# Two small tensors allocated ahead of the load ring of a one-token attention and MLP kernel

## The chip, the core and the metric

The kernel runs on one core of a Trainium2 chip, with the other cores idle. The metric is the device time of one execution in microseconds (us). The time before is the median of three runs, 2518.27 us, the lowest 2518.11 and the highest 2518.29.

The engines of the core are called PE (matrix multiplication; PEld is its weight load), DVE (vector), ACT (scalar), POOL and SP. SP does no arithmetic here: it issues the loads, which 16 DMA engines carry out. On-chip memory is SBUF, 128 partitions side by side, and PSUM, into which PE accumulates.

## What is computed

One token passes through an attention block with a cache of 65536 keys and values for each of 32 heads, and through a gated MLP; a gate mixes both.

```
q = (x @ wq) as 32 heads of 128
scores = q . k_cache * 128**-0.5          (32 heads x 65536 keys)
o = softmax(scores) . v_cache             (32 heads x 128)
a = o @ wo
b = (silu(x @ w_gate) * (x @ w_up)) @ w_down
g = sigmoid(sum(x * gate_w))
out = g * a + (1 - g) * b
```

All tensors are bf16. k_cache and v_cache hold 32 x 65536 x 128 elements each, 537 MB, and every byte of them is read once. The weights add 13.9 MB.

## The kernel before

**The ring.** One SBUF tensor, `ring` (line 74), takes all large loads: 176 KiB in each partition, cut by byte offsets into places. The first half of a head's K lies at K_A (0) and the second at K_B (32 KiB); with 64 KiB each they lie at 0 to 64 and at 32 to 96 KiB, so each is loaded into what the other has left. The two halves of V lie at V_A (96 KiB) and V_B (112 KiB) in the same way. wq comes first, at 144 KiB; wo, w_gate, w_up and w_down reuse the places of K at the end. `at(byte, n)` (line 119) gives the part of the ring from a byte offset on; all offsets are multiples of 256 bytes.

**The loads.** Each half of a head's K or V is 8 MiB: 256 rows of 128 bf16 in each of 128 partitions, that is one contiguous run of 64 KiB per partition in HBM and in SBUF. SP issues them in one queue, in the order written out at lines 142 to 197: for each head K's first half of the next head, V's second half, K's second half, V's first half, each after a wait for the engine that frees the place (`ktd` for K, counted up by DVE; `va1` and `vbd` for V, counted up by PE). In the first head K comes in four loads of 4 MiB. In the last, V's second half comes in six parts (PARTS, line 123), the first of them ahead of a wait for `va1`, and w_down in one large load and three small ones that follow the parts of V.

**The computing.** DVE transposes K chunk by chunk (`turn`, line 310; L314) from the ring into one of four buffers of `kt`, 16 chunks per half-head; PE multiplies each with the head's q, laid out in `zq` (L401), into scores in the bank psS. After a head's last chunk DVE takes the maximum (L338), POOL the maximum over the partitions (L216), ACT the exponential (L251), DVE transposes the weights into `pb` (L340), and PE multiplies V by them (L417 and L408). At the end come wo (L428 and L512), the MLP (L488 and after) and the sum into one row.

**The two small tensors.** `om` (line 85, 64 bytes per partition) holds the last-but-one set of attention outputs as weights for wo; ACT writes it once (L259), PE reads it in 32 matmuls (L428). `qTb` (line 97, 64 bytes per partition) holds q in bf16; ACT writes it once (L239), and PE reads it in 4 matmuls (L395).

**Where tensors lie.** SBUF tensors are laid out in the order in which `sb` (line 56) is called, one after the other, behind a scratch area of 16384 bytes and four small constants of 32 bytes each per partition. So `ring`, which is called first, begins at byte 16384 + 128 = 16512 of each partition.

## Time and profile before

| | |
|---|---|
| median of three runs | 2518.27 us |
| the profiled execution, its own time | 2518.01 us |
| its span, from first to last instruction | 2516.6 us |
| read from HBM | 1087.64 MB, 432 GB/s over the span |
| loads into the ring | 144, of which 125 are of 8 MiB |

The profile has a page with the busy times of the engines, the DMA queues and the chain of work that ended last, and a trace that can be asked for windows, waits and DMA packets. A DMA packet is one run of bytes into one partition; DMA share is the mean busy share of the 16 DMA engines. Chain rows give a start and a duration in us, and what took it. Rows of windows give the stretch and its length, then for each engine the busy time and the number of instructions, then the granted clock of PE as a share of full speed, the DMA share and the rate. In rows of groups come the line, engine and operation, what is written from what, the count, then the busy time, the mean of one in ns, and the idle time ahead of them with what ended it.

### The profile page before, as it was taken

What the parts mean: (1) busy time and instruction counts of PE and PEld (TensorE: products, weight loads), DVE (VectorE), ACT (ScalarE), POOL (GpSimd) and SP (SyncE); (2) the same over time, 40 slices, a digit from 0 to 9 for tenths busy, and PEclk for the clock granted to TensorE, in tenths of its full rate; (3) what the DMA queues carried; (4) which work ended last, traced back from release to release, by engine and by line L of the source; (5) the groups of instructions that cost most, each with busy time, mean ns of one, the idle gap of its engine ahead of it and who ended that gap; (6) DMA issues with size and microseconds to landing.
All of it is one profiled execution on the core that took longest, in us unless ns stands there. A gap on an engine that the chain in (4) does not pass through costs nothing.

```text
span 2516.6 us, 25250 instructions
## 1 busy us (share of the span) xinstructions
PE 1511.9 (60%) x10158; PEld 573.9 (23%) x10158; DVE 1249.7 (50%) x1213; ACT 43.0 (2%) x142; POOL 25.9 (1%) x81
## 2 busy tenths in 40 slices
PE   4565655745656556566565575565655655656568
PEld 1222222212222222222222121222212222212222
DVE  5454553644545536445455364464553644545534
ACT  0000000000000000000000000000000000000000
POOL 0000000000000000000000000000000000000000
PEclk8877877878778778778787787877877778778788
DMA  9999999999999999999999999999999999999999
GB/s 419 434 433 433 434 433 434 433 434 434 434 433 434 434 433 435 433 432 433 433 433 433 433 433 433 433 433 433 433 434 433 433 433 434 433 433 433 433 432 394
DMA packets 20748, 1087.73 MB, mean 432 GB/s; under 512 B 2307, under 2 KB 2694, under 8 KB 2950
## 3 DMA queue, kind: packets, MB, share of 16 engines
q1 hardware_dynamic: 20736, 1087.64, 99.9%
q8 instruction: 4, 0.07, 0.0%
q14 instruction: 2, 0.02, 0.0%
q10 hardware_dynamic: 6, 0.00, 0.0%
HBM read 1087.64 MB, written 0.00 MB: 432 GB/s over the span
## 4 chain that ended last, share of the span: by engine, by line
DMA 75%; DVE 15%; issue 7%; PE 2%; DVEq 1%; SPq 0%; ACT 0%; POOL 0%
DMA ring<-in_A_k_cache_dram 74%; DVE kt L314 15%; PE psS L401 2%; DMA ring<-in_A_v_cache_dram 1%; DVEq L311 0%; SPq L145 0%; PE psW L417 0%; DVE st L325 0%; PE psY L423 0%; ACT pa L251 0%; DVE pb L340 0%; DVE st L338 0%; DVEq L324 0%; DVE fin L359 0%; SPq L136 0%
## 5 line engine op out<-in xcount | busy, mean ns | idle before, releaser
L401 PE MATMUL psS<-kt,zq 128*128 128x512 bf16 x4096 | 1132.6, 425 | 854.6 <-DVE kt L314 835.3
L314 DVE STREAM_TRANSPOSE kt<-ring 128x1024 uint32<-128x1024 uint32 x1024 | 1163.1, 1206 | 939.7 <-DMA ring<-in_A_k_cache_dram 939.7
L401 PEld LDWEIGHTS psS<-kt,zq 128*128 128x128 bf16 x4096 | 385.1, 104 | 1588.3 <-DVE kt L314 1129.7
L417 PE MATMUL psW<-ring,pb 128*4 128x512 bf16 x3584 | 256.2, 448 | 102.7 <-DVE pb L340 102.4
L417 PEld LDWEIGHTS psW<-ring,pb 128*4 128x4 bf16 x3584 | 94.8, 98 | 262.6 <-issue 187.8
L327 DVE COPY brow<-psW 128x512 f32<-128x512 f32 x32 | 22.1, 691 | 120.5 <-PE psW L417 120.5
L408 PEld LDWEIGHTS psO<-pb,ring 128*128 128x128 bf16 x2048 | 57.0, 98 | 0.5 <-DMA ring<-in_A_v_cache_dram 0.2
L408 PE MATMUL psO<-pb,ring 128*128 128x1 bf16 x2048 | 56.6, 163 | 0.2
L330 DVE TENSOR_SCALAR lt<-psO,st,sc 128x4 f32 x32 | 9.4, 294 | 89.1 <-PE psO L408 89.1
L452 PE MATMUL psO<-id,brow 128*128 128x1 f32 x256 | 33.8, 253 | 25.5 <-DVE brow L327 24.7
L340 DVE STREAM_TRANSPOSE pb<-pa 128x512 bf16<-128x512 bf16 x32 | 22.8, 711 | 48.7 <-ACT pa L251 48.7
L249 ACT ACTIVATE st<-st 128x1 f32<-128x1 f32 x32 | 6.5, 203 | 2358.5 <-POOL st L216 2358.5
L338 DVE TENSOR_REDUCE st<-psS 128x1 f32<-128x512 f32 x32 | 22.1, 692 | 37.4 <-PE psS L401 37.4
L452 PEld LDWEIGHTS psO<-id,brow 128*128 128x128 f32 x256 | 31.0, 191 | 41.7 <-DVE brow L327 40.4
L216 POOL PARTITION_ALL_REDUCE st<-st x32 | 11.2, 351 | 2420.2 <-DVE st L338 2420.2
L251 ACT ACTIVATE pa<-psS,st 128x512 bf16<-128x512 f32 x32 | 22.0, 687 | 1.0
L428 PE MATMUL psF<-ring,om 128*1 (+1 forms) x32 | 12.7, 396 | 2.9 <-DMA ring<-in_A_wo_dram 2.9
L512 PE MATMUL psY<-ring,hot 128*128 (+1 forms) x32 | 13.1, 411 | 0.0
L218 POOL PARTITION_ALL_REDUCE st<-st x32 | 12.3, 383 | 36.4 <-ACT pa L251 36.4
L256 ACT COPY zq<-qd 128x16 bf16 x31 | 7.7, 248 | 0.0
L251 ACT ACTIVATION_READ_ACCUMULATOR pa<-psS,st 128x1 f32 x32 | 6.2, 193 | 0.0
L428 PE MATMUL psF<-ring,kt 128*1 128x512 bf16 x11 | 4.2, 564 | 3.0 <-DVE kt L353 3.0
(87 smaller groups left out, 52.8 us busy)
## 6 DMA issues: line engine op xcount, KB each, us to landing
ring<-in_A_k_cache_dram SPq DMA_DIRECT2D x4, 4096.0 KB, 27.4
ring<-in_A_v_cache_dram SPq DMA_DIRECT2D x3, 2048.0 KB, 17.6
ring<-in_A_wq_dram SPq DMA_DIRECT2D x1, 4096.0 KB, 12.4
ring<-in_A_wo_dram SPq DMA_DIRECT2D x2, 2048.0 KB, 10.6
ring<-in_B_w_gate_dram SPq DMA_DIRECT2D x1, 1792.0 KB, 21.4
ring<-in_B_w_up_dram SPq DMA_DIRECT2D x1, 1792.0 KB, 25.4
ring<-in_B_w_down_dram SPq DMA_DIRECT2D x1, 1408.0 KB, 13.1
ring<-in_A_v_cache_dram SPq DMA_DIRECT2D x1, 1280.0 KB, 20.4
```

Of the source, the lines that this page charges most:

```text
L218: nc.gpsimd.partition_all_reduce(Lt, rsum, P, RADD).then_inc(sm["s_L"], 1)
L251: nc.scalar.activation(pa[:], psS[:], ACT.Exp, bias=nbias, scale=SCALE, accum_out=rsum).then_inc(sm["s_exp"], 1)
L314: nc.vector.transpose(o, src).then_inc(sm["ktd"], 1)
L327: nc.vector.tensor_copy(brow[:], psW[:]).then_inc(sm["s_flc"], 1)
L338: nc.vector.reduce_max(mxs, psS[:], AX_X).then_inc(sm["s_mx"], 1)
L340: nc.vector.transpose(pb[:], pa[:]).then_inc(sm["s_pb"], 1)
L401: last = nc.tensor.matmul(psS[:], zw[je][c], ktb[n % NB][:, je // 2, :, je % 2], start=first and je == 0, stop=stop and je == 3)
L408: last = nc.tensor.matmul(psO[:, 0:1], at(base + r * 256, Dh), pb[:, col:col + 1], start=first and n == 0, stop=stop and n == len(rows) - 1)
L417: last = nc.tensor.matmul(psW[g:g + 4, :], pb[:, col:col + 97:32], at(base + r * 256, 4 * Dh), start=first and n < 4, stop=stop and n >= l ...
L428: return nc.tensor.matmul(psF[0:1, :], lhs, rhs, start=first, stop=stop)
L452: nc.tensor.matmul(psO[:, 0:1], brow[:, e * Dh:(e + 1) * Dh], id4[:, e:e + 1], start=e == 0, stop=False)
L512: return nc.tensor.matmul(psY[:], hot[:, bass.ds(31 - j, P)], w, start=first, stop=stop)
```

## The change

`om` and `qTb` are allocated ahead of `ring` instead of behind it. With 64 bytes each in a partition they move the ring from byte 16512 to byte 16640 of each partition. The tensors from `kt` to `hot` move by 128 bytes too, those from `o31` to `xTz` by 64, and `hbuf` and `st` keep their place. The instructions of all engines, their order and their waits are the same; only addresses differ.

```
+        om = sb("om", [P, 32], BF16)
+        qTb = sb("qTb", [P, H], BF16)
         ring = sb("ring", [P, RING // 2], BF16)
...
         hot = sb("hot", [P, P + 32], BF16)
-        om = sb("om", [P, 32], BF16)
         o31 = sb("o31", [P, 2], BF16)
...
         xTz = sb("xTz", [P, 4 * 32], BF16)
-        qTb = sb("qTb", [P, H], BF16)
         hbuf = sb("hbuf", [P, 5, 16], F32)
```

More of the change, by code (lines that the diff above doesn't have):

```diff
@@ L72, in bass_gated_mix__mha_block_cached__swiglu_ffn__decode_kernel @@
         psF = psum("psF", [P, 512], F32)
+        om = sb("om", [P, 32], BF16)
+        qTb = sb("qTb", [P, H], BF16)
         ring = sb("ring", [P, RING // 2], BF16)
@@ L84, in bass_gated_mix__mha_block_cached__swiglu_ffn__decode_kernel @@
         hot = sb("hot", [P, P + 32], BF16)
-        om = sb("om", [P, 32], BF16)
         o31 = sb("o31", [P, 2], BF16)
@@ L96, in bass_gated_mix__mha_block_cached__swiglu_ffn__decode_kernel @@
         xTz = sb("xTz", [P, 4 * 32], BF16)
-        qTb = sb("qTb", [P, H], BF16)
         hbuf = sb("hbuf", [P, 5, 16], F32)
```

## The prediction

> **What bounds the kernel now.** I read the page's first lines, its waits and its chain, then the DMA answers for chosen windows.

> ```profile
> span 2516.6 us, 25250 instructions
> PE 1511.9 (60%) x10158; PEld 573.9 (23%) x10158; DVE 1249.7 (50%) x1213; ACT 43.0 (2%) x142; POOL 25.9 (1%) x81
> DMA  9999999999999999999999999999999999999999
> DMA packets 20748, 1087.73 MB, mean 432 GB/s; under 512 B 2307, under 2 KB 2694, under 8 KB 2950
> q1 hardware_dynamic: 20736, 1087.64, 99.9%
> DMA 75%; DVE 15%; issue 7%; PE 2%; DVEq 1%; SPq 0%; ACT 0%; POOL 0%
> ```

> The 16 DMA engines are busy from end to end, with one queue, q1, which holds all loads that SP issues. No compute engine passes 60%. The chain that ended last is three quarters DMA; the rest of it is DVE, PE and issue time in which the chain has stepped over to the work that released the next load, while the DMA engines stayed busy with the one before. That they stayed busy shows in the steady part, taken as six equal windows, of which the first and the last stand here (PE, PEld, DVE, ACT, POOL, then granted clock, DMA share and GB/s):

> ```profile
> 100.00:487.00 387.00, 228.72 (x1565) 89.05 (x1563) 193.66 (x186) 5.65 (x20) 3.67 (x10) 0.77 1.00 434
> 2035.00:2422.00 387.00, 230.87 (x1565) 87.56 (x1563) 193.64 (x186) 5.64 (x20) 3.67 (x10) 0.78 1.00 434
> ```

> So the time of the steady part is (bytes through q1) / (rate of q1), and only what changes that rate can move it. The waits say the same from the other side:

> ```profile
> DVE kt L314 <- DMA ring<-in_A_k_cache_dram: 939.7, 65, 22.6
> SPq L145 <- DVE kt L314: 1369.6, 65, 30.7
> ring<-in_A_v_cache_dram SPq DMA_DIRECT2D x63, 32.4
> ring<-in_A_k_cache_dram SPq DMA_DIRECT2D x62, 29.3
> ```

> DVE idles 939.7 us for K, 14.5 us in each of its 65 waits. SP too waits a great deal before it issues, but a load lands 29.3 or 32.4 us after its issue, and its own bytes need 19.35 us (worked out next): each load is issued some 10 us before its turn, and the queue does not run dry.

> The exact rate comes from two rows of the chain of waits, both K loads of the same phase of a head:

> ```profile
> 62.44 29.26 DMA ring<-in_A_k_cache_dram
> 2268.47 29.23 DMA ring<-in_A_k_cache_dram
> ```

> Between them lie 57 half-heads, each with one K and one V load of 8 MiB: (2268.47 - 62.44) / 57 = 38.702 us for 16.777 MB, 433.5 GB/s. One load takes 19.351 us, and in it each of the 16 DMA engines writes 8 packets of 64 KiB and one small packet that raises the semaphore (q1 has 20736 packets = 144 loads x (128 + 16); the 16 x 144 = 2304 small ones are nearly all of the 2307 under 512 B).

> **How much of a packet is not its bytes.** A change of start address can touch what a packet costs beside its bytes. The trace gives that by comparing long packets with short ones. At the end the queue moves rows of 1 KiB:

> ```profile
> DMA packets 126, 0.11 MB, mean 36 GB/s; under 512 B 16, under 2 KB 126, under 8 KB 126
> q1 hardware_dynamic: 126, 0.11, 10.5%
> ```

> This is the window from 2512.9 to 2516 us: 110 packets of 1 KiB and 16 small ones took 10.5% of 16 x 3.1 us = 5208 ns. With a cost c for each packet and a rate r of one engine, 126c + 112640/r = 5208 here, and 9c + 524288/r = 19351 in the steady part. The solution is c = 8.5 ns and r = 27.2 bytes per ns. The 10.5% is rounded, which leaves c open by 0.2 ns. So of the 2419 ns from one 64 KiB packet to the next, 2409 are bytes and 8.5 are c.

> **The change part by part.**

> *The ring.* In the built programs' tables of tensors the ring begins at byte 16512 of each partition before (64 x 256 + 128) and at 16640 after (65 x 256). Every load into it starts at a whole multiple of 256 bytes from the ring's start (16 K, 32 K, r0*256, 1024j), so before the change every data packet begins 128 bytes into a 256-byte block and ends 128 bytes into another; afterwards each one covers whole blocks. The same 144 loads with the same packets are issued, behind the same waits; no instruction is added, removed or reordered on any engine, SP's queue among them.

> No row of before shows a load into an aligned ring, so the gain per packet is bounded from two sides. One end is nothing: c may have no part that depends on the address. The other is the whole c, 8.5 ns. I take 4.7 ns, close to the middle: the time that the 128 unused bytes of the first block would need at r, 128 / 27.2. That is the cost if a packet that begins inside a block pays for the whole block. Below nothing, I bound it by the same amount with the other sign (in the rivals).

> [...]

> How many packets count: each load puts 8 data packets on each engine. The last three loads (1 KiB rows of w_down) are issued behind the last part of V and are not what the chain waits for. That leaves 141 x 8 = 1128 packets in a row on each engine. Gain: 1128 x 4.7 ns = 5.3 us; the ends are 0 and 1128 x 8.5 ns = 9.6 us.

> *Does the gain reach the end?* In the steady part yes: the queue always has the next load, and 0.04 us less per load (8 x 4.7 ns) is nothing beside the 10 us of lead. In the tail SP has to wait for PE before it issues the last parts of V:

> ```profile
> 2432.53 29.84 DMA ring<-in_A_k_cache_dram
> 2484.96 5.32 PE psW L417 x37
> 2492.09 21.33 DMA ring<-in_A_v_cache_dram
> 2513.46 0.37 PE psO L408 x8
> 2492.00:2493.00 1.00, 1.00 (x12) 0.27 (x8) 0.00 (x0) 0.00 (x0) 0.00 (x0) 1.00 1.00 424
> ```

> The last K load lands at 2462.4; compute then sets the moment of that issue, 2490 to 2492. It moves forward with the landing of K, by the 1048 packets before it (131 loads x 8), 4.9 us. In the meantime the engines work off the loads already queued, five of them with 40 packets each engine (V's first half, w_gate, w_up, w_down, the first part of V's second half), which now end 0.2 us earlier relative to K. They are still at full share at 2492, and from there 21.3 us pass until the last part lands, of which the 48 KiB per partition issued there need 14.5 us: some 5 us of older work is ahead of them. So the queue still does not run dry, and the full 5.3 us arrive at the landing at 2513.4. The 3.2 us from there to the end stay.

> *The other moved tensors.* kt, zq, qd, pa, pb, lt, ident, sel, ramp and hot move by 128 bytes, o31 to xTz by 64, and om and qTb to the front. All moves are multiples of 64 bytes, the shapes stay.

> ```profile
> L314 DVE STREAM_TRANSPOSE kt<-ring 128x1024 uint32<-128x1024 uint32 x1024 | 1163.1, 1206 | 939.7 <-DMA ring<-in_A_k_cache_dram 939.7
> L401 PE MATMUL psS<-kt,zq 128*128 128x512 bf16 x4096 | 1132.6, 425 | 854.6 <-DVE kt L314 835.3
> L428 PE MATMUL psF<-ring,om 128*1 (+1 forms) x32 | 12.7, 396 | 2.9 <-DMA ring<-in_A_wo_dram 2.9
> ```

> I cost these at nothing. The cover is DMA: the transposes may lengthen by a tenth (16 x 0.12 = 1.9 us in a half-head) and still fit in the 14.5 us that DVE waits there. If the cover were gone, that tenth would cost 64 x 1.9 = 123 us, so a shift of this kind would be seen at once in the mean of L314. The matmuls that read om are 12.7 us in all, while the last K load and V's first half are in flight; a tenth of them would be 1.3 us.

> *The sum.* Profiled execution: span 2516.6, 2518.0 with the 1.4 us around it. 2516.6 - 5.3 + 1.4 = 2512.7. The median of the three runs is 2518.3, 0.3 above the profiled one, so the forecast for the median is 2513.0 us. With 0.5 ns of doubt on the 4.7 its own range is 2512.4 to 2513.6.

> **The rivals.**

> *Nothing changes.* c is a packet's own cost, whatever its address. For it speaks the small packet that raises a semaphore, seen alone in the 20 ns from 2516.17 us:

> ```profile
> q10 hardware_dynamic: 1, 0.00, 2.8%
> ```

> 2.8% of 16 x 20 ns is 9.0 ns for 4 bytes, which need 0.15 ns at r. It has nothing to do with the ring and costs as much beside its bytes as a data packet does. Against it: a write of 4 bytes fills its own block only in part too, so it may pay in the same way. Time: 2518.3, with 0.3 either way.

> *The whole c goes.* A packet that starts and ends inside blocks may pay at both ends, and twice 4.7 ns is already more than c. Then 9.6 us are saved: 2518.3 - 9.6 = 2508.7. Against it: some time between two packets is needed for any address, as the semaphore's packet suggests.

> *Slower: the blocks are counted from another origin.* The offset is counted from the start of a partition. If a partition's first byte stood 128 bytes into a block of the memory that DMA writes, the ring would be aligned today and misaligned by the change. Place: the first block of each data packet; price: 128 / 27.2 = 4.7 ns on each, c becomes 13.2; it decides from the first load on, since nothing hides the queue: 2518.3 + 5.3 = 2523.6. For it: nothing in the trace shows the origin, and a c of 8.5 ns can be had without any misalignment, as the semaphore's packet shows. Against it: the partition's 16 KiB and the tensors' offsets are all counted from zero, and a start at an odd 128 would be a strange one.

> **How the numbers follow.** Half a block saved, 0.55; nothing, 0.25; the whole c, 0.10; slower by half a block, 0.10. The likeliest gives 2513.0. The range takes in nothing and the bound of c: 2508.5 to 2518.8, which leaves out the slower case and little else. A change of 0.2% is 5.0 us (about what a measurement of this kernel can tell from no change), so the line runs at 2513.2, just above the forecast: of the first case I count three quarters as faster. Faster 0.42 + 0.10 = 0.52; same 0.13 + 0.24 = 0.37; slower 0.11.

> **What would show it.** If right, K loads in the chain stand 38.626 us per half-head apart instead of 38.702 (two loads, 16 packets, 4.7 ns each), the same pair of rows 4.3 us closer, the 1 KiB window gives a c near 3.8 ns, the first K load lands less than 0.1 us earlier (16 packets), and DVE's and PE's mean durations at L314 and L401 stay. If the pitch stays at 38.70, c is the packet's own. If the pitch shrinks and the time does not, the gain is lost in the tail between 2462 and 2492. What would make all of it wrong is a change in r itself, above all a pitch that moves by more than 0.14 us per half-head, which c cannot give.

## The result and the profile after

The changed kernel takes 2513.71 us (median of 21 runs, 2513.45 to 2514.49), against 2518.29 us in 21 runs of the kernel before (2518.03 to 2519.19). The ratio is 0.9982, with a 95% interval of 0.9975 to 0.9988: 4.6 us faster. The forecast was 2513.0, a gain of 5.3 us. The median lies 0.1 us above the range of the forecast's own case (2512.4 to 2513.6) and inside the whole range (2508.5 to 2518.8).

The page of the changed kernel, with the span, the DMA packets, the queue and two groups (busy time, mean in ns | idle time before them):

```profile
span 2512.5 us, 25250 instructions
DMA packets 20749, 1087.73 MB, mean 433 GB/s; under 512 B 2308, under 2 KB 2695, under 8 KB 2951
q1 hardware_dynamic: 20736, 1087.64, 100.0%
L401 PE MATMUL psS<-kt,zq 128*128 128x512 bf16 x4096 | 1132.7, 426 | 851.7 <-DVE kt L314 833.2
L314 DVE STREAM_TRANSPOSE kt<-ring 128x1024 uint32<-128x1024 uint32 x1024 | 1163.1, 1206 | 936.4 <-DMA ring<-in_A_k_cache_dram 936.4
```

The queue q1 moves the same number of packets as before (20736), the transposes and matmuls are as long as before (1206 ns, 426 against 425), and DVE waits 3.3 us less for K. Only the queue has become faster. By how much is read in the chain of waits, from issues of K an even number of half-heads apart. The time per half-head is called the pitch:

```profile
62.40 29.18 DMA ring<-in_A_k_cache_dram
139.63 29.54 DMA ring<-in_A_k_cache_dram
178.66 29.11 DMA ring<-in_A_k_cache_dram
217.19 29.29 DMA ring<-in_A_k_cache_dram
2226.38 29.26 DMA ring<-in_A_k_cache_dram
2265.12 29.11 DMA ring<-in_A_k_cache_dram
```

From 217.19 to 2226.38 lie 52 half-heads: a pitch of 38.638 us. Before, the even pair is 62.44 and 2229.72, the latter in the next fence:

```profile
2191.07 29.22 DMA ring<-in_A_k_cache_dram
2229.72 29.27 DMA ring<-in_A_k_cache_dram
2268.47 29.23 DMA ring<-in_A_k_cache_dram
```

This gives 2167.28 / 56 = 38.701 us. The reader should take pairs an even number apart, because half-heads alternate: 38.65 and 38.75 us before (the last three rows), 38.53 and 38.74 after. The prediction called its pair, 57 apart, one of the same phase; it isn't, and that cost it 0.001 us.

The gain is 0.063 us per half-head, 3.9 ns on each of the 16 packets. By the medians it is 4.58 us / 1128 packets = 4.06 ns. The span of the profiled execution shrank by less, 4.1 us. Part of the rest stands in the rows above: the half-head from 139.63 took 39.03 us, against 38.74 in the run with a pad ahead of the ring, shown below, whose addresses are as good. So it is a matter of this execution.

The tail of the chain in the changed kernel:

```profile
2428.91 29.82 DMA ring<-in_A_k_cache_dram
2481.32 4.48 PE psW L417 x48
2487.61 21.73 DMA ring<-in_A_v_cache_dram
2509.38 0.36 PE psO L408 x8
```

The last K lands at 2458.7 instead of 2462.4, V's last part at 2509.3 instead of 2513.4, and 3.2 us remain after it as before. Nothing of the gain is lost there: the last stretch gains some 0.4 us more than K's landing did.

### The profile page after: what moved, and what is told of

Same layout as the page of the kernel before. It is cut to its first block, busy times and chain, and to the rows that moved or that the text cites. A ratio compares the mean times of both kernels' runs of the same rounds, so it can differ in the third digit from the quotient of the medians.

```text
span 2512.5 us, 25250 instructions
## 1 busy us (share of the span) xinstructions
PE 1510.1 (60%) x10158; PEld 574.4 (23%) x10158; DVE 1249.7 (50%) x1213; ACT 43.0 (2%) x142; POOL 25.9 (1%) x81
## 2 busy tenths in 40 slices
DMA  9999999999999999999999999999999999999999
DMA packets 20749, 1087.73 MB, mean 433 GB/s; under 512 B 2308, under 2 KB 2695, under 8 KB 2951
## 3 DMA queue, kind: packets, MB, share of 16 engines
q1 hardware_dynamic: 20736, 1087.64, 100.0%
HBM read 1087.64 MB, written 0.00 MB: 433 GB/s over the span
## 4 chain that ended last, share of the span: by engine, by line
DMA 75%; DVE 15%; issue 7%; PE 2%; DVEq 0%; SPq 0%; ACT 0%; POOL 0%
DMA ring<-in_A_k_cache_dram 74%; DVE kt L314 15%; PE psS L401 2%; DMA ring<-in_A_v_cache_dram 1%; DVEq L311 0%; SPq L145 0%; PE psW L417 0%; DVE st L325 0%; PE psY L423 0%; ACT pa L251 0%; DVE pb L340 0%; DVE st L338 0%; DVEq L324 0%; DVE fin L359 0%; SPq L136 0%
## 5 line engine op out<-in xcount | busy, mean ns | idle before, releaser
L401 PE MATMUL psS<-kt,zq 128*128 128x512 bf16 x4096 | 1132.7, 426 | 851.7 <-DVE kt L314 833.2
L314 DVE STREAM_TRANSPOSE kt<-ring 128x1024 uint32<-128x1024 uint32 x1024 | 1163.1, 1206 | 936.4 <-DMA ring<-in_A_k_cache_dram 936.4
L401 PEld LDWEIGHTS psS<-kt,zq 128*128 128x128 bf16 x4096 | 386.8, 104 | 1583.9 <-DVE kt L314 1120.7
L417 PE MATMUL psW<-ring,pb 128*4 128x512 bf16 x3584 | 253.5, 444 | 103.5 <-DVE pb L340 102.4
L417 PEld LDWEIGHTS psW<-ring,pb 128*4 128x4 bf16 x3584 | 93.9, 97 | 261.3 <-issue 184.4
L408 PEld LDWEIGHTS psO<-pb,ring 128*128 128x128 bf16 x2048 | 56.8, 98 | 0.6 <-DMA ring<-in_A_v_cache_dram 0.6
L408 PE MATMUL psO<-pb,ring 128*128 128x1 bf16 x2048 | 56.5, 163 | 0.4 <-DMA ring<-in_A_v_cache_dram 0.2
L428 PE MATMUL psF<-ring,om 128*1 (+1 forms) x32 | 13.1, 410 | 2.7 <-DMA ring<-in_A_wo_dram 2.7
L428 PE MATMUL psF<-ring,kt 128*1 128x512 bf16 x11 | 4.0, 542 | 2.9 <-DVE kt L353 2.9
## 6 DMA issues: line engine op xcount, KB each, us to landing
ring<-in_A_wo_dram SPq DMA_DIRECT2D x2, 2048.0 KB, 10.5
```

The costliest lines, as they stand in the source:

```text
L314: nc.vector.transpose(o, src).then_inc(sm["ktd"], 1)
L401: last = nc.tensor.matmul(psS[:], zw[je][c], ktb[n % NB][:, je // 2, :, je % 2], start=first and je == 0, stop=stop and je == 3)
L408: last = nc.tensor.matmul(psO[:, 0:1], at(base + r * 256, Dh), pb[:, col:col + 1], start=first and n == 0, stop=stop and n == len(rows) - 1)
L417: last = nc.tensor.matmul(psW[g:g + 4, :], pb[:, col:col + 97:32], at(base + r * 256, 4 * Dh), start=first and n < 4, stop=stop and n >= l ...
L428: return nc.tensor.matmul(psF[0:1, :], lhs, rhs, start=first, stop=stop)
```

## The experiments

The runs that differ by a pad are the kernel before with an unused tensor of so many bytes per partition, ahead of the ring where nothing else is said. Prices per packet are taken against 2513.71 us, with 1128 packets.

**The ring by a pad.** The pad moves the ring, and everything behind it by the same 128 bytes; `om` and `qTb` stay behind the ring.

```
+        pad = sb("pad", [P, 64], BF16)
         ring = sb("ring", [P, RING // 2], BF16)
```

> The ring moves by 128 bytes behind an unused pad, with om and qTb where they were; all tensors behind the ring move by 128 too. Theory (the ring's place alone does it): the time of the changed kernel, 2513.7 us, steady pitch of K loads 38.64 us per half-head. Rival (om or qTb at the front matter): 2518.3 or between.

Measured: 2513.64 us, ratio 0.9982 (0.9973 to 0.9991). Its chain:

```profile
62.50 29.19 DMA ring<-in_A_k_cache_dram
139.71 29.26 DMA ring<-in_A_k_cache_dram
178.45 29.09 DMA ring<-in_A_k_cache_dram
2226.12 29.26 DMA ring<-in_A_k_cache_dram
2264.87 29.11 DMA ring<-in_A_k_cache_dram
2428.67 29.64 DMA ring<-in_A_k_cache_dram
```

2163.62 / 56 = 38.636 us per half-head, and here from the start on (139.71 to 178.45 is 38.74). Any 128 bytes would do in the place of `om` and `qTb`: their own new place does nothing.

**The rest alone.** The same pad, behind the ring.

```
         ring = sb("ring", [P, RING // 2], BF16)
+        pad = sb("pad", [P, 64], BF16)
         kt = sb("kt", [P, NB, CH * 64], U32)
```

> The pad stands behind the ring: the ring stays at 128 bytes into a block, all tensors behind it move by 128. Theory (the ring's place): no gain, 2518.3 us, pitch 38.70. Rival (kt, zq or another tensor behind the ring gains by its multiple of 256): 2513.7, or a mean of L314 or L401 that moves.

Measured: 2518.15 us, ratio 0.9998 (0.9989 to 1.0007), and this chain:

```profile
62.80 29.29 DMA ring<-in_A_k_cache_dram
2230.10 29.28 DMA ring<-in_A_k_cache_dram
```

2167.30 / 56 = 38.702 us, the pitch of before. The gain belongs to the ring's place.

**The ring at 192 and at 32 bytes into a block** (pads of 64 and of 160 bytes).

> The ring starts 192 bytes into a 256-byte block. Theory A (a packet pays for the unused bytes of its first block, here 192 instead of 128): half as much again as the cost measured at 128 (4.1 ns a packet), 6.1 ns, so 2513.7 + 6.9 = 2520.6 us. Theory B (one more transaction, whatever the offset): 2518.3 us. Theory C (blocks of 64 bytes or less count): 2513.7 us.

Measured: 2518.35 us, ratio 1.0000 (0.9991 to 1.0009): 4.1 ns a packet.

> The ring starts 32 bytes into a 256-byte block. Theory A (unused bytes of the first block): a quarter of the cost at 128, 1.0 ns a packet, 2513.7 + 1.2 = 2514.9 us. Theory B (one more transaction, whatever the offset): 2518.3 us. Unused bytes of the last block instead (224 of 256): 7.2 ns, 2521.8 us.

Measured: 2519.44 us, ratio 1.0005 (0.9996 to 1.0014): 5.1 ns a packet. Its chain:

```profile
62.69 29.30 DMA ring<-in_A_k_cache_dram
2230.97 29.30 DMA ring<-in_A_k_cache_dram
```

2168.28 / 56 = 38.719 us. Theory A, on which the size of the prediction rested, falls at both: the unused bytes of the first block were 192 and 32, a factor of six, and the price came out the other way round. The unused bytes of the last block do no better, with 64 at the first and 224 at the second. What is left is theory B, one price for a packet that does not start on the block, with something on top at 32. All packets are whole blocks long, except the small ones, so one that starts off the block also ends off it; these runs can't tell the two ends apart.

**At 64 and at 224 bytes** (pads of 192 and of 96).

> The ring starts 64 bytes into a 256-byte block. The runs at 128 (2518.3) and 192 (2518.35) speak for one price at any offset, the run at 32 (2519.44) for a higher one there. If the rest to 64 bytes adds a price of its own: 2518.3 here. If the first bytes of a block matter by their number (32, 64, 128 falling): between, near 2519.0.

> The ring starts 224 bytes into a 256-byte block. If an offset that is no multiple of 64 adds a price of its own, whichever end it stands at: 2519.4 us, as at 32. If it falls with the offset: 2518.3 us or less. Theory A of the runs before (unused bytes of the first block, 224 of 256), which those runs have already left little room: 2521.8.

Measured: 2518.43 us at 64, ratio 1.0000 (0.9991 to 1.0009), 4.2 ns; 2519.53 us at 224, ratio 1.0005 (0.9996 to 1.0014), 5.2 ns. So offsets fall into two groups:

```
offset in 256 bytes   us        ns per packet
0                     2513.7    0
64                    2518.4    4.2
128                   2518.3    4.1
192                   2518.4    4.1
32                    2519.4    5.1
224                   2519.5    5.2
```

The step of 1.1 us between the groups is within the intervals of the single ratios. It is held up by the pitch, which repeats itself within each group: 38.704 us at 64 (from 62.93 to 2230.35 in the chain, 56 half-heads), 38.705 at 192 (62.52 to 2230.02), 38.719 at 32 and 38.720 at 224 (62.62 to 2230.92). What sets 32 and 224 apart is open: both are no multiple of 64, and both stand 32 bytes from the edge of a block. An offset of 96 or 160 bytes would tell these apart and was not run.

The records of the single packets in the traces show the same groups directly. The packets of 64 KiB that start between 100 and 2400 us took, in the mean, 2418.0 ns with the pad that puts the ring on a block, 2421.7 at 128 bytes, 2421.8 at 64, 2421.9 at 192, and 2422.65 at 32 and at 224. So the records hold 3.7 of the 4.1 ns, and most of the 1 ns on top. They also show that the price is a mean: with the pad 99.8% of the packets took 2418 ns, while at 128 bytes 16% took that long too and 23% took 2425 to 2427 ns.

**A multiple of 512** (a pad of 384 bytes).

> The ring starts at byte 16896, a multiple of 512 as well (16640 is one of 256 alone). Theory (blocks of 256): as the changed kernel, 2513.7 us, pitch 38.64. Rival (blocks of 512, of which the change used half): below, by up to what it gained, down to 2509.

Measured: 2513.82 us, ratio 0.9982 (0.9973 to 0.9991). A start on a multiple of 512 (16896) gives nothing beyond one on a multiple of 256 alone (16640, 2513.71 us).

**The sources shifted.** Loads of the first halves, all but the first K, read from 128 bytes further on, so the output is that of shifted keys and values:

```
+                if u == 0:
+                    flat = {"k": A_k_cache, "v": A_v_cache}[kind][0].rearrange("h s d -> h (s d)")
+                    src = flat[:, Dh // 2:Dh // 2 + S * Dh // 2].rearrange("h (p n) -> h p n", p=P)
```

> The changed kernel, with the sources of the first halves of K and V (all but the first head's K) read from 128 bytes further on in HBM, so the output is that of shifted keys and values: half of the packets start inside a block in HBM while the ring is aligned. Theory (only the destination counts): 2513.7 us. Rival 1 (source and destination must stand alike in their blocks): half of the gain goes, 2516.0 us. Rival 2 (a read pays for its block by itself): also 2516.0 us; the next run tells these two apart.

Measured: 2513.72 us, ratio 0.9982 (0.9973 to 0.9991).

> The kernel before, with the same shift of the sources by 128 bytes for the first halves, the output again that of shifted keys and values: half of the packets now start 128 bytes into a block at both ends. Theory (only the destination counts): 2518.3 us. Rival 1 (alike in their blocks is enough): half of the gain, 2516.0 us. Rival 2 (a read pays for its block by itself, beside the write): 2518.3 + 2.3 = 2520.6 us.

Measured: 2518.28 us, ratio 1.0000 (0.9991 to 1.0009). Neither moved by as much as 0.1 us, where the rivals asked for 2.3, taking half of the packets as shifted (63 of 141 loads were, which makes 2.1). It is the start in SBUF that counts; the start in HBM does not, by 128 bytes, and the two need not agree. Other shifts of the source were not tried.

**More packets for the same bytes.** 94 loads are cut in two, on the changed kernel and on the kernel before (the waits of DVE and PE count on accordingly):

```
-                load(at(byte, ROWS * Dh), src, s)
+                if s == "s_vb":
+                    load(at(byte, ROWS * Dh), src, s)
+                else:
+                    for x in range(2):
+                        load(at(byte + x * ROWS * Dh, ROWS * Dh // 2), src[:, x * half:(x + 1) * half], s)
```

> The changed kernel with 94 of its 8 MiB loads (all whole-half loads of K, and V's first halves) cut into two of 4 MiB: 752 more data packets and 94 more semaphore packets on each engine for the same bytes. Theory (an aligned packet costs about 4.8 ns beside its bytes, as the steady pitch of 19.319 us per load leaves it at 27.2 bytes per ns): 846 x 4.8 ns = 4.1 us more than the changed kernel, 2517.8 us. Rival (8.5 ns, the c that the prediction solved for, which an aligned packet still shows in the 1 KiB rows): 7.2 us more, 2520.9.

Measured: 2517.72 us, ratio to the kernel before 0.9997 (0.9988 to 1.0006); 4.01 us above the changed kernel. For 846 packets that is 4.7 ns each, if a packet that raises a semaphore costs as much as one of data, which the run can't tell.

> The kernel before with the same loads cut in two. Theory (the offset is paid once by each packet, 4.0 ns whatever its length): the distance to the run of the changed kernel cut in the same way grows from 4.6 us to 4.6 + 752 x 4.0 ns = 7.6 us, so 2525.4 us if that run takes 2517.8. Rival (the offset lowers the rate of the bytes): the distance stays 4.6 us, 2522.4.

Measured: 2525.59 us, ratio 1.0029 (1.0018 to 1.0040), 7.9 us above the cut changed kernel where the uncut ones are 4.6 apart. The 752 more data packets brought 3.3 us of that, 4.4 ns each, at half the length. The rival with the rate of the bytes, which kept the distance at 4.6 us, falls. The page of this run shows the packets that were added, and its chain the pitch:

```profile
DMA packets 34284, 1087.74 MB, mean 431 GB/s; under 512 B 3811, under 2 KB 4198, under 8 KB 4454
q1 hardware_dynamic: 34272, 1087.65, 100.1%
```

```profile
63.58 28.46 DMA ring<-in_A_k_cache_dram
2237.04 28.79 DMA ring<-in_A_k_cache_dram
```

34272 - 20736 = 13536 = 16 x 846. The pitch is 2173.46 / 56 = 38.812 us, 0.111 above that of before, and the packets of 32 KiB are paid like those of 64. Their records say the same: 1217.0 ns in the mean here, 1213.0 in the cut changed kernel.

## Why the prediction came out right, step by step

*What bounds the kernel.* Right. The queue is full in both kernels (q1 99.9% before, 100.0% after), and the time follows its pitch: 0.063 us x 64 half-heads is 4.0 us, and the 104 packets of the other loads add 0.4 at the same price, of 4.6 measured. The pitch was forecast to fall by 0.076 us.

*How much of a packet is not its bytes.* The value for before was about right: from the two cut runs an aligned packet costs 4.7 ns, and one at 128 bytes (2525.59 - 2518.34 us less 94 x 4.7 ns) / 752, that is 9.0 ns against the 8.5 on record. That the two agree is luck, as the same working after the change shows. The prediction expected the rows of 1 KiB to give about 3.8 ns after the change. The window from 2508.8 to 2511.9 us of the changed kernel says:

```profile
DMA packets 112, 0.10 MB, mean 33 GB/s; under 512 B 15, under 2 KB 109, under 8 KB 112
q1 hardware_dynamic: 112, 0.10, 9.5%
```

94 packets of 1 KiB, 3 of 2 KiB and 15 small ones took 4712 ns. Solved with 19319 ns per load as in the prediction, this gives c = 8.5 ns again, where the cut run gives 4.7. Two things were wrong in the reading. First, the last rows of 1 KiB did not pay for the offset: in the records the 110 of the prediction's window took 46.0 ns each before the change, as all 384 do after it, while all 384 had a mean of 47.7 before. Second, the recorded time is not the cost in the queue, because the records of packets that follow each other overlap. The sign of that stood in the trace of before all the time, in the window from 100 to 2422 us:

```profile
q1 hardware_dynamic: 17279, 1006.58, 100.2%
```

More than 100% busy means that the recorded times add up to more than the time there was. Unrounded it is 0.16%, some 60 us over 17279 packets, 3.5 ns each; after the change it is 3.4. So a packet's whole cost must come from the distance between loads, or from changing the number of packets. The difference that an address makes does show in the records, since the overlap is about the same in both.

*The ring.* The place and the sign were right, and the size nearly, with 4.7 ns forecast and 4.1 measured. The size came near by luck. The step that failed is the reason for the 4.7: "a packet that begins inside a block pays for the whole block" by its unused bytes. The runs show a price that does not follow the unused bytes: 4.1 to 4.2 ns at 64, 128 and 192 bytes, and 5.1 to 5.2 at 32 and 224. At 128 bytes the wrong rule and the right price lie 0.6 ns apart; at 32 the wrong one would have been short by 4 ns, at 224 over by 3. What the price consists of is not shown. A packet of 64 KiB that starts off a block touches 257 blocks instead of 256, which fits that all five offsets cost something, but that is argued. It explains neither the 1 ns on top at 32 and 224 nor that some packets at 128 bytes took no longer than aligned ones.

That blocks of 256 bytes count was the author's assumption; nothing in the profile of before shows it. The runs do: the starts at an odd and at an even multiple of 256 (bytes 16640 and 16896) took 2513.7 and 2513.8 us, and the five offsets between multiples 2518.3 to 2519.5.

*How many packets.* Right: the pitch gives 3.9 ns a packet in the changed kernel and 4.1 in the run with the pad (38.701 less 38.638 or 38.636 us, over 16), so 1128 packets make 4.4 to 4.6 us, and 4.6 were measured.

*Whether the gain reaches the end.* Right. The last K was forecast 4.9 us earlier. It is 4.1 in the run with the pad ahead of the ring (2428.67 + 29.64 against 2462.37), 1048 packets at 3.9 ns, and 3.6 in the profiled changed kernel with its slow half-head.

*The other moved tensors.* Right. The run that moved all tensors behind the ring by 128 bytes, and not the ring, gained nothing, and the run with the pad gained as much with `om` and `qTb` behind the ring as the change does with them ahead of it.

*The rivals.* Nothing changes: fallen, though its argument holds half: 4.7 ns do belong to a packet in the kernel with the aligned ring (4.01 us for the 846 that the cut added). How much of the 9.0 ns on record for a semaphore's packet is its own cost, and how much overlap, is not shown. The whole c: fallen, for the same reason. Slower through another origin: fallen; the starts at multiples of 256, counted from the start of a partition (16640 and 16896, 2513.7 and 2513.8 us), are the cheap ones.

*The threshold.* The gain of 0.18% came out just short of the 0.2% from which the prediction counts a change as faster, where its forecast of 5.3 us lay just beyond; the interval, 0.12 to 0.25%, reaches to both sides.

No run beat the changed kernel by more than 0.1 us: with it, the four with an aligned ring and uncut loads lie between 2513.64 and 2513.82 us.

## What to carry to other kernels

Where a full DMA queue sets the time, look up the start byte of the load buffers in a partition and try a multiple of 256; here 128 bytes ahead did it, as `om` and `qTb` (2513.71 us) or as an unused pad (2513.64), and it was worth 4 ns for each packet on each engine. The gain is by the packet, 0.2% with rows of 64 KiB, and with rows of 32 KiB it was 4.4 ns a packet. No run here puts a full queue of short rows to the test; the last rows of 1 KiB show 1.7 ns in their records (47.7 and 46.0). The number of packets is a second handle: with the ring aligned, each of the 846 that the cut added cost 4.7 ns; no run took packets away. Settle the whole cost of a packet by changing the number of packets, since the recorded durations overlap by some 3.5 ns, nearly as much as the effect; for an address, compare the mean duration between two kernels.
